# Retention then a bilinear FFN on one core: casts of two chunks moved ahead, four chunks of attention spread out, last rows stored in halves

## The chip, the core and the metric

One core of a Trainium2 chip runs the whole program. The metric is the device time of one execution in microseconds (us); the runs of the kernel before have a median of 350.2 us. A ratio below is the mean time of one kernel's fast runs over the mean of the other's fast runs of the same rounds, so it is not quite the ratio of the medians that are quoted. Spans in the profile (first to last instruction) are some 1.7 us shorter than the times.

Names used by the profile: PE is TensorE's matmuls, PEld its weight loads, DVE VectorE, ACT ScalarE, POOL GpSimd, SP SyncE, which issues most DMAs here. Tiles in its lines: qkb are q and k as bf16, tp and qkT their transposes, sc the scores, sT the masked scores, o the outputs of the attention, xT the FFN's input, pa and pb the FFN's first two products, po its last one, and osb the copy of po that is stored. A copy out of po is called an eviction.

## The reference

```python
def _attn_ref(q, k, v):                       # 8 batches, 8 heads, 576 positions, head size 64
    scores = np.matmul(q, k.transpose(0, 1, 3, 2)) / np.sqrt(64)
    rel = pos[:, None] - pos[None, :]
    Dmat = np.where(rel >= 0, gamma[:, None, None] ** rel[None], 0.0)   # decay, causal
    return np.matmul(scores * Dmat, v)

def _moe_ref(x, w_a, w_b, w_out):             # 4608 tokens, 512 -> 1536 -> 512
    return ((x @ w_a) * (x @ w_b)) @ w_out
```

The attention is linear (no softmax), so it can be done in chunks of 128 tokens with a running state: per chunk, `state` adds k'v to a matrix, `scores` makes q k' of the chunk itself, a mask job on DVE zeroes the non-causal half, `outputs` adds state and chunk, and an xT job on DVE scales the result into the FFN's input.

## The kernel before

The 36 chunks' attention is woven into the FFN's stream of matmuls. The FFN runs in blocks of tokens (512, 256, 384, 384, then 512 each); a generator yields after each matmul with its cost in units of a 512-column matmul, and the schedule runs its next entry when the running sum `at` has passed that entry's place and the stream is at an edge. Entries placed between edges slip to the next one: every 4 units in block 0's second half and in block 1's first, every 6 in the first half of the 384-token block.

```python
    def cast(i, on="pool"):              # q, k to bf16; v scaled to bf16
        ...
        if on == "pool": nc.gpsimd.tensor_copy(qb, qf)
        else:            nc.scalar.copy(qb, qf)
        if on == "dve":  nc.vector.tensor_copy(kb, kf)
        else:            nc.gpsimd.tensor_copy(kb, kf)
        ...
    def turn(i):                         # chunks 6 and up: q, k transposed by DMA, issued by SP
        ...
        nc.sync.dma_start_transpose(qkT..., natural[i][0]...)
    def transposes(i):                   # chunks 0 to 5: on TensorE, through PSUM
        ...
    def scores(i):
        ...
        later.append(lambda: masked(0))  # DVE jobs, run by pop() at places in the FFN's stream
        later.append(lambda: masked(1))
    ...
    def ahead(upto, on="pool"):
        while counts["cast"] <= min(upto, NCH - 1):
            i = counts["cast"]
            cast(i, on)
            counts["cast"] += 1
            if i >= FIRST_TURNED:                     # 6
                turn(i)
            if i >= FIRST_TURNED + 1 and counts["load"] < NCH:
                load(counts["load"])                  # q, k, v of a chunk 2 further on
                counts["load"] += 1

    def one_by_one(what, i):
        if what == "T":
            ahead(i, "dve")
            transposes(i)
        elif what == "S":
            scores(i)
            flush()
            state(i)
        else:
            flush()
            outputs(i)                                # leaves its xT job in `later`

    for i, first, second, third in ((4, 117, 122, 128), (5, 132, 135, 140)):
        todo += [(first, one_by_one, ("T", i)), (second, one_by_one, ("S", i)),
                 (third, one_by_one, ("A", i))]
    placed = [((6, 7), 145, 178, 194), ((8,), 166, 197, 207),
              ((9, 10), 186, 230, 250)]
    ...                                               # chunks 11 to 35: places worked back from
        placed.append((g, third - 104, third - 36, third))    # where their block starts
```

`later` is a list of DVE jobs; `pop()` starts one at the end of each pb group and twice per row block of po, `flush()` starts all. Each engine's queue is worked through in order: in the trace of before, the k cast of chunk 4 (48.37 us, its data there since 45.12) follows the eviction in front of it (47.76).

Of the kernel before, what the change touches and what calls it, by code (L numbers as in the profile page):

```python
# [10 lines left out]
FP32 = mybir.dt.float32  # L11
# [7 lines left out]
def kernel(  # L19
# [19 lines left out]
    nc = tc.nc  # L39

    B, H, S, D = q.shape
    DM = H * D
    DFF = moe_w_a.shape[1]
    NTOK = B * S
    NC = DM // 128
    NF = DFF // 128
# [10 lines left out]
    def rows_of(i):  # L57

        b, m = 2 * (i // PER), i % PER
        if m < MID:  # L60
            return [(0, 128, b, 128 * m)]
        if m == MID:
            return [(0, 64, b, 128 * m), (64, 64, b + 1, 0)]
        return [(0, 128, b + 1, 64 + 128 * (m - MID - 1))]

    def pool(name, bufs, space=None):
        kw = {} if space is None else {"space": space}
        return ctx.enter_context(tc.tile_pool(name=name, bufs=bufs, **kw))
# [11 lines left out]
    ps_ffn = pool("ps_ffn", 3, PS)  # L80
# [10 lines left out]
    wo_sb = big.tile([128, NF, DM], BF16)  # L91
# [18 lines left out]
    for i in range(4):  # L110
# [18 lines left out]
        out=mask, in_=mask, compare_op=ALU.is_ge, fill=0.0,  # L129
# [44 lines left out]
    def pop():  # L174
        if later:
            later.pop(0)()

    def flush():
        while later:
            later.pop(0)()  # L180
# [22 lines left out]
    def turn(i):  # L203

        qkT = qkt_pool.tile([128, 2, HP, 128], BF16, tag="qkT", name="qkT")
        nc.sync.dma_start_transpose(
            qkT.rearrange("p w c s -> p (w c) s"),
            natural[i][0].rearrange("p w d -> p (w d)"))
        transposed[i] = qkT

    def transposes(i):

        natural_qk = natural[i][1:3]
        qkT = qkt_pool.tile([128, 2, HP, 128], BF16, tag="qkT", name="qkT")
        for w, copy in ((0, nc.scalar.copy), (1, nc.vector.tensor_copy)):
            tp = ps_att.tile([128, HP, 128], BF16, tag="att", name="tp")
            for p in range(HP):
                nc.tensor.transpose(tp[:, p, :],  # L218
                                    natural_qk[w][:, p * 128:(p + 1) * 128],
                                    identity)  # L220
            copy(qkT[:, w], tp)
        transposed[i] = qkT
# [43 lines left out]
    def outputs(i, halves=False):  # L266
        m = i % PER
        qkb, qb, kb, vb = natural.pop(i)
        qkT = transposed.pop(i)
        sT = scored.pop(i)  # L270
        o = ps_att.tile([128, HP, 128], FP32, tag="att", name="o")
        if m > 0:
            st = state_of.pop(i)
            n = 64 if m == MID else 128
            for p in range(HP):
                for hi in (0, 1):
                    nc.tensor.matmul(o[64 * hi:64 * hi + 64, p, 0:n],  # L277
                                     st[:, p, 64 * hi:64 * hi + 64],
                                     qkT[:, 0, p, 0:n],
                                     start=(p == 0), stop=True,  # L280
                                     skip_group_check=True)
        for p in range(HP):
            for hi in (0, 1):
                e0 = p * 128 + 64 * hi
                nc.tensor.matmul(o[64 * hi:64 * hi + 64, p, :],  # L285
                                 vb[:, e0:e0 + 64], sT[:, hi, p, :],
                                 start=(m == 0 and p == 0), stop=True,
                                 skip_group_check=True)
        s0 = rows_of(i)[0][3]

        def scaled(c0, c1):
            nc.vector.tensor_tensor(  # L292
                xT[:, c0:c1, i * 128:(i + 1) * 128], o[:, c0:c1],
                qs[:, c0:c1, s0:s0 + 128], op=ALU.mult)

        if halves:
            later.append(lambda: scaled(0, HP // 2))
            later.append(lambda: scaled(HP // 2, HP))
        else:
            later.append(lambda: scaled(0, HP))  # L300
# [5 lines left out]
    def ffn_block(tok0, n, runs):  # L306

        hT = h_pool.tile([128, NF, 512], BF16, tag="h", name="hT")
        f0 = 0
        for count in runs:  # L310
            has = {}
            for F in range(f0, f0 + count):
                fs = slice(F * 128, (F + 1) * 128)
                pa = ps_ffn.tile([128, 512], FP32, tag="ab", name="pa")
                for c in range(NC):
                    nc.tensor.matmul(pa[:, 0:n], wa_sb[:, c, fs],  # L316
                                     xT[:, c, tok0:tok0 + n],
                                     start=(c == 0), stop=(c == NC - 1))
                    if c < NC - 1:
                        yield n / 512, False  # L320
                ha = ha_pool.tile([128, 512], BF16, tag="ha", name="ha")
                nc.scalar.copy(ha[:, 0:n], pa[:, 0:n])  # L322
                has[F] = ha
                yield n / 512, False
            for F in range(f0, f0 + count):
                fs = slice(F * 128, (F + 1) * 128)
                pb = ps_ffn.tile([128, 512], FP32, tag="ab", name="pb")
                for c in range(NC):
                    nc.tensor.matmul(pb[:, 0:n], wb_sb[:, c, fs],  # L329
                                     xT[:, c, tok0:tok0 + n],  # L330
                                     start=(c == 0), stop=(c == NC - 1))
                    if c < NC - 1:
                        yield n / 512, False
                nc.vector.tensor_tensor(hT[:, F, 0:n], has[F][:, 0:n],  # L334
                                        pb[:, 0:n], op=ALU.mult)
                pop()
                yield n / 512, True
            f0 += count
        for u in range(n // 128):
            po = ps_ffn.tile([128, 512], FP32, tag="ab", name="po")  # L340
            for F in range(NF):
                nc.tensor.matmul(po, hT[:, F, u * 128:(u + 1) * 128],  # L342
                                 wo_sb[:, F, :],
                                 start=(F == 0), stop=(F == NF - 1))
                if F == 5:
                    pop()
                if F < NF - 1:
                    yield 1.0, F % 4 == 3
            osb = o_pool.tile([128, DM], FP32, tag="osb", name="osb")
            if u % 2 == 0:  # L350
                nc.scalar.copy(osb, po)  # L351
            else:
                nc.vector.tensor_copy(osb, po)  # L353
            nc.sync.dma_start(
                out[tok0 + u * 128:tok0 + (u + 1) * 128, :], osb)
            pop()
            yield 1.0, True


    gate = const.tile([1, 64], BF16)  # L360
# [48 lines left out]
    starts, at = {}, 0.0  # L409
# [10 lines left out]
# [5 lines that stand above are left out]
            if i >= FIRST_TURNED:  # L425
                turn(i)
            if i >= FIRST_TURNED + 1 and counts["load"] < NCH:
                load(counts["load"])
                counts["load"] += 1
# [13 lines left out]
            outputs(i)  # L443

    def one_by_one(what, i):
        if what == "T":
            ahead(i, "dve")
            transposes(i)
        elif what == "S":
            scores(i)  # L450
            flush()
            state(i)
        else:
            flush()
            outputs(i)

    todo = []
    for i, first, second, third in ((4, 117, 122, 128), (5, 132, 135, 140)):
        todo += [(first, one_by_one, ("T", i)), (second, one_by_one, ("S", i)),
                 (third, one_by_one, ("A", i))]  # L460
    placed = [((6, 7), 145, 178, 194), ((8,), 166, 197, 207),
              ((9, 10), 186, 230, 250)]
    limit = 1e9
    for i in range(NCH - 1, 10, -2):
        g = (i, i + 1) if i + 1 < NCH else (i,)
        third = min(starts[i] - 16, limit - 60)
        limit = third
        placed.append((g, third - 104, third - 36, third))
    for g, zeroth, second, third in placed:
        todo += [(zeroth, ahead, (g[-1],)), (second - 14, first_stage, (g,)),  # L470
                 (second, second_stage, (g,)), (third, third_stage, (g,))]
# [2 lines left out]
    at = 0.0  # L474
    tok = 0
    for tb, n in enumerate(blocks):
        runs = WCOLS if tb == 0 else [1] * NF
        for cost, edge in ffn_block(tok, n, runs):
            at += cost
            while todo and edge and at >= todo[0][0]:  # L480
                _, fn, args = todo.pop(0)
                fn(*args)
        flush()
        tok += n
# [30 lines left out]
```

## Time and profile before

| of the kernel before | |
|---|---|
| time, median (lowest to highest of 4) | 350.22 us (350.19 to 352.2) |
| PE busy | 331.2 us of a span of 348.7 |
| start-up until the first FFN matmul | 21.66 us |
| from the end of the last matmul to the end of the span | 3.98 us |

The view by stretches of time shows where PE was not full. The columns are the stretch, its length, then busy us of PE, PEld, DVE, ACT and POOL with their numbers of instructions, the granted TensorE clock, the mean share of DMA engines busy (over 1 where packets overlap) and GB/s.

```profile
43.00:62.00 19.00, 15.53 (x134) 8.21 (x133) 7.53 (x14) 5.37 (x12) 8.09 (x11) 1.00 1.18 234
62.00:96.00 34.00, 31.97 (x325) 21.59 (x323) 18.75 (x35) 12.74 (x32) 12.72 (x17) 1.00 1.27 192
96.00:320.00 224.00, 224.00 (x1599) 111.81 (x1598) 106.11 (x166) 67.62 (x134) 49.23 (x65) 1.00 0.68 135
```

In the first row 3.5 us of PE are idle, in the second 2.0, in the third nothing in 224 us. The DMA share is above 1 in the first two rows and 0.68 in the third: the stretch with the holes is also the one in which the DMA engines are busy throughout.

### The profile page before, as it was taken

What the parts mean: (1) busy time and instruction counts of PE and PEld (TensorE: products, weight loads), DVE (VectorE), ACT (ScalarE), POOL (GpSimd) and SP (SyncE); (2) the same over time, 40 slices, a digit from 0 to 9 for tenths busy, and PEclk for the clock granted to TensorE, in tenths of its full rate; (3) what the DMA queues carried; (4) which work ended last, traced back from release to release, by engine and by line L of the source; (5) the groups of instructions that cost most, each with busy time, mean ns of one, the idle gap of its engine ahead of it and who ended that gap; (6) DMA issues with size and microseconds to landing.
All of it is one profiled execution on the core that took longest, in us unless ns stands there. A gap on an engine that the chain in (4) does not pass through costs nothing.

```text
span 348.7 us, 6143 instructions
## 1 busy us (share of the span) xinstructions
PE 331.2 (95%) x2414; PEld 170.7 (49%) x2414; DVE 160.9 (46%) x272; ACT 111.8 (32%) x228; POOL 85.0 (24%) x121
## 2 busy tenths in 40 slices
PE   2989987999799999999999999999999999999995
PEld 1544443866455654444444444444544444444442
DVE  5644334474664363365336533653365236513421
ACT  8522322514323342333142404240423143213320
POOL 4660035235333441220233023401331110000000
PEclk9999999999999999999999999999999999999999
DMA  9999999999999991930995099708990950020002
GB/s 175 191 196 208 206 209 250 211 201 187 186 220 232 218 229 62 212 59 3 223 264 116 2 204 268 133 0 160 251 196 0 155 149 2 0 92 30 0 32 90
DMA packets 154189, 50.74 MB, mean 146 GB/s; under 512 B 144944, under 2 KB 149552, under 8 KB 154160
## 3 DMA queue, kind: packets, MB, share of 16 engines
q1 hardware_dynamic: 149408, 45.63, 69.3%
q0 software_dynamic: 4752, 4.72, 8.4%
q8 instruction: 19, 0.31, 0.4%
q14 instruction: 10, 0.08, 0.1%
HBM read 37.75 MB, written 9.44 MB: 135 GB/s over the span
## 4 chain that ended last, share of the span: by engine, by line
PE 90%; DVE 3%; SPq 2%; POOL 2%; DMA 1%; issue 1%; ACT 0%; DVEq 0%
PE pa L316 27%; PE po L342 27%; PE pb L329 27%; PE o L277 2%; PE o L285 2%; SPq L104 2%; PE kv L235 2%; DMA vf<-in_v_dram 1%; DVE sT L258 1%; DVE hT L334 1%; POOL vb L196 1%; POOL wa_sb L163 1%; DVE xT L292 0%; POOL wb_sb L164 0%; DVE osb L353 0%
## 5 line engine op out<-in xcount | busy, mean ns | idle before, releaser
L334 DVE TENSOR_TENSOR hT<-ha,pb 128x512 bf16<-128x512 bf16 (+2 forms) x120 | 76.1, 634 | 107.3 <-PE pb L329 105.3
L316 PE MATMUL pa<-xT,wa_sb 128*128 128x512 bf16 (+2 forms) x480 | 111.7, 358 | 1.9 <-DVE xT L292 1.9
L329 PE MATMUL pb<-xT,wb_sb 128*128 128x512 bf16 (+2 forms) x480 | 111.5, 358 | 0.0
L322 ACT CAST ha<-pa 128x512 bf16<-128x512 f32 (+2 forms) x120 | 65.1, 542 | 125.7 <-PE pa L316 114.0
L342 PE MATMUL po<-wo_sb,hT 128*128 128x512 bf16 x432 | 98.0, 379 | 0.0
L329 PEld LDWEIGHTS <-wb_sb 128*128 128x128 bf16 x480 | 47.0, 98 | 46.5
L316 PEld LDWEIGHTS <-wa_sb 128*128 128x128 bf16 x480 | 45.1, 98 | 45.0 <-issue 2.2
L342 PEld LDWEIGHTS <-hT 128*128 128x128 bf16 x432 | 40.5, 98 | 47.1
L196 POOL TENSOR_TENSOR vb<-vf,vs 128x512 bf16<-128x512 f32 x36 | 37.5, 1042 | 58.9 <-DMA vf<-in_v_dram 44.8
L189 POOL CAST qkb<-qf 128x512 bf16<-128x512 f32 x30 | 18.3, 610 | 114.0 <-DMA qf<-in_q_dram 94.7
L353 DVE COPY osb<-po 128x512 f32<-128x512 f32 x17 | 11.8, 692 | 54.3 <-PE po L342 54.3
L351 ACT COPY osb<-po 128x512 f32<-128x512 f32 x19 | 11.1, 585 | 74.5 <-PE po L342 74.5
L292 DVE TENSOR_TENSOR xT<-o,qs 128x512 bf16<-128x512 f32 (+1 forms) x37 | 24.2, 671 | 9.5 <-PE o L285 9.2
L195 POOL CAST qkb<-kf 128x512 bf16<-128x512 f32 x32 | 19.6, 613 | 22.0 <-DMA kf<-in_k_dram 21.9
L285 PE MATMUL o<-sT,vb 128*64 128x128 bf16 x288 | 14.7, 222 | 1.3 <-DVE sT L258 1.3
L218 PE MATMUL tp<-identity,qkb 128*128 128x128 bf16 x48 | 5.6, 263 | 8.4 <-ACT qkb L191 6.8
L235 PE MATMUL kv<-vb,qkb 128*128 128x128 bf16 (+1 forms) x128 | 12.8, 224 | 0.7 <-POOL vb L196 0.7
L235 PEld LDWEIGHTS <-qkb 128*128 128x128 bf16 (+1 forms) x128 | 9.5, 99 | 7.1 <-issue 1.9
L285 PEld LDWEIGHTS <-vb 128*64 128x64 bf16 x288 | 10.3, 111 | 2.7 <-issue 2.3
L252 PEld LDWEIGHTS <-qkT 64*128 64x128 bf16 x288 | 8.6, 96 | 5.9 <-issue 1.9
L218 PEld LDWEIGHTS <-qkb 128*128 128x128 bf16 x48 | 3.8, 116 | 11.0 <-ACT qkb L191 7.6
L240 ACT CAST state_165<-kv 64x256 bf16<-64x256 f32 x8 | 2.9, 365 | 7.5 <-PE kv L235 7.5
(195 smaller groups left out, 155.4 us busy)
## 6 DMA issues: line engine op xcount, KB each, us to landing
out_dram<-osb SPq DMA_DIRECT2D x36, 256.0 KB, 3.1
qf<-in_q_dram SPq DMA_DIRECT2D x32, 256.0 KB, 4.0
kf<-in_k_dram SPq DMA_DIRECT2D x32, 256.0 KB, 4.6
vf<-in_v_dram SPq DMA_DIRECT2D x32, 256.0 KB, 4.9
wo_sb<-in_moe_w_out_dram POOLq DMA_DIRECT2D x3, 512.0 KB, 17.2
qf<-in_q_dram SPq DMA_DIRECT2D x8, 128.0 KB, 4.5
kf<-in_k_dram SPq DMA_DIRECT2D x8, 128.0 KB, 5.0
vf<-in_v_dram SPq DMA_DIRECT2D x8, 128.0 KB, 4.5
```

Of the source, the lines that this page charges most:

```text
L189: nc.gpsimd.tensor_copy(qb, qf)
L195: nc.gpsimd.tensor_copy(kb, kf)
L196: nc.gpsimd.tensor_tensor(vb.rearrange("p (h d) -> p h d", h=H), vf.rearrange("p (h d) -> p h d", h=H), vs[:, i % PER, :].unsqueeze(2).to_ ...
L235: nc.tensor.matmul(kv[:, p, :], kb[r, sl], vb[r, sl], start=(m in (0, MID) and p == 0), stop=True, skip_group_check=True)
L285: nc.tensor.matmul(o[64 * hi:64 * hi + 64, p, :], vb[:, e0:e0 + 64], sT[:, hi, p, :], start=(m == 0 and p == 0), stop=True, skip_group_che ...
L292: nc.vector.tensor_tensor(xT[:, c0:c1, i * 128:(i + 1) * 128], o[:, c0:c1], qs[:, c0:c1, s0:s0 + 128], op=ALU.mult)
L316: nc.tensor.matmul(pa[:, 0:n], wa_sb[:, c, fs], xT[:, c, tok0:tok0 + n], start=(c == 0), stop=(c == NC - 1))
L322: nc.scalar.copy(ha[:, 0:n], pa[:, 0:n])
L329: nc.tensor.matmul(pb[:, 0:n], wb_sb[:, c, fs], xT[:, c, tok0:tok0 + n], start=(c == 0), stop=(c == NC - 1))
L334: nc.vector.tensor_tensor(hT[:, F, 0:n], has[F][:, 0:n], pb[:, 0:n], op=ALU.mult)
L342: nc.tensor.matmul(po, hT[:, F, u * 128:(u + 1) * 128], wo_sb[:, F, :], start=(F == 0), stop=(F == NF - 1))
L353: nc.vector.tensor_copy(osb, po)
```

## The change

Its intent is to remove the known waits: casts ahead of the evictions that delayed them, the result of a single chunk evacuated at once, one more step of the FFN between scores and outputs of chunks 9 and 10 (so that the masks are ready), and a shorter tail. The core of the diff:

```diff
-            po = ps_ffn.tile([128, 512], FP32, tag="ab", name="po")
...
+            final = rows.stop == NTOK
+            for part in range(2 if final else 1):
+                cols = (slice(part * DM // 2, (part + 1) * DM // 2) if final
+                        else slice(0, DM))
...          # matmuls, eviction and store of `cols` alone; the last half is evicted by ScalarE
     def one_by_one(what, i):
-        if what == "T":
+        if what == "C":
             ahead(i, "dve")
+        elif what == "T":
             transposes(i)
...
             flush()
             outputs(i)
+            flush()
-    for i, first, second, third in ((4, 117, 122, 128), (5, 132, 135, 140)):
...
+    for i, places in ((4, (110, 117, 121, 127)), (5, (127, 132, 136, 139))):
+        todo += [(at, one_by_one, (what, i))
+                 for at, what in zip(places, "CTSA")]
...
-              ((9, 10), 186, 230, 250)]
+              ((9, 10), 186, 224, 254)]
...
-        placed.append((g, third - 104, third - 36, third))
+        placed.append((g, third - 104, third - (30 if i == 11 else 36), third))
```

More of the change, by code (lines that the diff above doesn't have):

```diff
@@ L339, in ffn_block @@
         for u in range(n // 128):
-            po = ps_ffn.tile([128, 512], FP32, tag="ab", name="po")
-            for F in range(NF):
-                nc.tensor.matmul(po, hT[:, F, u * 128:(u + 1) * 128],
-                                 wo_sb[:, F, :],
-                                 start=(F == 0), stop=(F == NF - 1))
-                if F == 5:
-                    pop()
-                if F < NF - 1:
-                    yield 1.0, F % 4 == 3
-            osb = o_pool.tile([128, DM], FP32, tag="osb", name="osb")
-            if u % 2 == 0:
-                nc.scalar.copy(osb, po)
-            else:
-                nc.vector.tensor_copy(osb, po)
-            nc.sync.dma_start(
-                out[tok0 + u * 128:tok0 + (u + 1) * 128, :], osb)
-            pop()
-            yield 1.0, True
+            rows = slice(tok0 + u * 128, tok0 + (u + 1) * 128)
+            final = rows.stop == NTOK
+            osb = o_pool.tile([128, DM], FP32, tag="osb", name="osb")
+            for part in range(2 if final else 1):
+                cols = (slice(part * DM // 2, (part + 1) * DM // 2) if final
+                        else slice(0, DM))
+                po = ps_ffn.tile([128, 512], FP32, tag="ab", name="po")
+                width = cols.stop - cols.start
+                for F in range(NF):
+                    nc.tensor.matmul(po[:, 0:width],
+                                     hT[:, F, u * 128:(u + 1) * 128],
+                                     wo_sb[:, F, cols],
+                                     start=(F == 0), stop=(F == NF - 1))
+                    if F == 5:
+                        pop()
+                    if F < NF - 1:
+                        yield width / 512, F % 4 == 3
+                if (u + part) % 2 == 0:
+                    nc.scalar.copy(osb[:, cols], po[:, 0:width])
+                else:
+                    nc.vector.tensor_copy(osb[:, cols], po[:, 0:width])
+                nc.sync.dma_start(out[rows, cols], osb[:, cols])
+                pop()
+                yield width / 512, True
     gate = const.tile([1, 64], BF16)
@@ L455, in one_by_one @@
             outputs(i)
+            flush()
     todo = []
-    for i, first, second, third in ((4, 117, 122, 128), (5, 132, 135, 140)):
-        todo += [(first, one_by_one, ("T", i)), (second, one_by_one, ("S", i)),
-                 (third, one_by_one, ("A", i))]
+    for i, places in ((4, (110, 117, 121, 127)), (5, (127, 132, 136, 139))):
+        todo += [(at, one_by_one, (what, i))
+                 for at, what in zip(places, "CTSA")]
     placed = [((6, 7), 145, 178, 194), ((8,), 166, 197, 207),
-              ((9, 10), 186, 230, 250)]
+              ((9, 10), 186, 224, 254)]
     limit = 1e9
```

## The prediction

> **What bounds the kernel now.** I read the page's busy shares and slices first, then the table of waits of TensorE (PE), then the order of time around each wait, then the DMA rows. The page:
>
> ```profile
> PE 331.2 (95%) x2414; PEld 170.7 (49%) x2414; DVE 160.9 (46%) x272; ACT 111.8 (32%) x228; POOL 85.0 (24%) x121
> ...
> PE   2989987999799999999999999999999999999995
> ...
> DMA  9999999999999991930995099708990950020002
> ```
>
> PE is the engine that bounds the kernel: full from about 96 us to the last slice, at the full granted clock. Its holes lie in the start-up, in slices 5 to 10 (44 to 96 us), and in the last slice. The DMA row is full until about 130 us, and that will matter. The waits of PE between 20 and 120 us:
>
> ```profile
> PE pa L316 <- DVE xT L292: 1.9, 2, 1.4
> PE o L285 <- DVE sT L258: 1.3, 3, 0.7
> PE tp L218 <- ACT qkb L191: 1.2, 1, 1.2
> PE tp L218 <- DVE qkb L193: 0.9, 1, 0.9
> PE sc_1389 L252 <- DVE xT L292: 0.7, 1, 0.7
> ```
>
> That is 6.0 us of idle PE, the whole reservoir of the scheduling part. Idle is measured from the modelled end of a matmul; from start to start, less the normal interval (0.216 us for 512 columns), the same holes lose more: 1.06 us (second transposes of chunk 4), 1.36 (transposes of chunk 5), 1.54 (first pa of block 1), 0.91+0.54 (outputs of chunk 10), 0.88 (scores of chunk 12), 0.68 (first pa of all), and 0.35 and 0.11; together 7.4 us after 20 us. I use these losses. Why the first three exist, in order of time:
>
> ```profile
> 47.76 0.69 DVE L353 COPY osb<-po 128x512 f32<-128x512 f32 x1 [4.42 <-PE po L342]
> 48.37 0.42 DVE L193 CAST qkb<-kf 128x512 bf16<-128x512 f32 x1
> 48.84 0.40 PE L218 MATMUL tp<-identity,qkb 128*128 128x128 bf16 x4 [0.90 <-DVE qkb L193]
> ...
> 53.26 0.58 ACT L351 COPY osb<-po 128x512 f32<-128x512 f32 x1 [1.82 <-PE po L342]
> 53.74 0.62 ACT L191 CAST qkb<-qf 128x512 bf16<-128x512 f32 x1
> 54.41 0.62 PE L218 MATMUL tp<-identity,qkb 128*128 128x128 bf16 x8 [1.20 <-ACT qkb L191]
> ...
> 59.00 0.69 DVE L353 COPY osb<-po 128x512 f32<-128x512 f32 x1 [1.45 <-PE po L342]
> 59.60 0.68 DVE L292 TENSOR_TENSOR xT<-o,qs 128x512 bf16<-128x512 f32 x1
> 60.34 0.60 PE L316 MATMUL pa<-xT,wa_sb 128*128 128x256 bf16 x4 [1.38 <-DVE xT L292]
> ```
>
> Each time a short job that PE needs at once (a cast, the last xT) sits in an in-order queue behind an eviction that itself waits for PE to finish a row of po. The cast's data was there long before: the records of landings have kf of chunk 4 at 45.12 us and of chunk 5 at 48.79.
>
> **What the Trainium skill says.** "Perfetto Trace Analysis", Identifying the Most-Contended Engine, warns that matmul busy share is no good measure of distance from roofline; so here, 95% busy hides losses larger than the idle time shown. Its section What "DMA-bound" means names, as one case, the issuing sequencer's track being solid DMA slices: the trace agrees, SyncE's issues follow each other from 36.8 to 95 us with gaps up to 0.6 us, and 144944 of 154189 packets are under 512 B. "TensorE: Matmul & The Clock Gate", Back-to-back issue gap, gives N/2.4+2.5 ns, so two 256-column matmuls (109 ns each) cost what one of 512 does (216); the trace agrees: four 256-column pa start every 0.43 us, weight loads included. "VectorE: DVE Perf Modes", The TRN2 errata, gives (172+N)/1.2 ns for ScalarE out of PSUM, 357 ns at 256 columns; the trace has 372 for the 256-column cast.
>
> **The change part by part.**
>
> *Casts ahead (chunks 4, 5).* The schedule acts only at multiples of 4 matmuls in this phase, so casts move from 120 to 112 and from 132 to 128; T, S and A stay at 120, 124, 128 and 132, 136, 140. Chunk 4: the k cast now precedes the eviction, runs near 45.3, and the 1.06 us goes. The next risk is the k copy of the transposes, behind the eviction: 48.45+0.42 = 48.85, when PE reaches the scores at 48.95. Chunk 5: ScalarE is free after the state copies (51.44, now 1.06 earlier), so q is cast by 51.0; DVE does xT of chunk 4 first (51.23 to 51.92), then the k cast to 52.25, needed at 52.20. So 1.36 shrinks to about 0.1.
>
> *Evacuated at once.* xT of chunk 5 no longer waits for the eviction of row block 3: outputs end about 55.64, xT at 56.35, PE needs it at 56.43. The 1.54 goes. Sum at the start of block 1: 1.06+1.26+1.54 = 3.9 us early (56.4 for 60.34).
>
> *Chunks 9 to 12.* Scores of 9 and 10 move from matmul 234 to 228, outputs from 252 to 258; both places fall on multiples of 6. Four mask jobs are popped one per step. Before, the fourth came only with the flush:
>
> ```profile
> 90.30 0.68 DVE L258 TENSOR_TENSOR sT<-sc_1232,mask 128x512 bf16<-128x512 f32 x1
> 90.44 0.22 PE L285 MATMUL o<-sT,vb 128*64 128x128 bf16 x1 [0.75 <-DVE sT L258]
> ```
>
> Now five steps (234 to 258) take four masks, each 0.56+0.68 us of DVE in a step of 1.30: 0.91+0.54 = 1.45 us goes. Scores of 11 and 12 move from 264 to 270, as far behind the outputs of 9 and 10 as before, so the 0.88 wait for xT stays by itself.
>
> *Last rows in halves.* PE time is the same (24 x 0.108 for 12 x 0.216). The tail is now eviction 0.69, issue and landing 2.00 (345.48 to 347.48, records of landings), end 1.2. The last eviction becomes ScalarE on 256 columns, about 0.37: -0.32. Half the bytes: the four stores of 56.8 us land 0.62 apart, so half a store is about 0.3 less at best; I take -0.25. Sum -0.57.
>
> Without anything else: 3.9+1.45+0.57 = 5.9 us.
>
> **What takes part of it back.** From chunk 6 on, qkT comes by DMA transposes, and that stream never waits for PE in this stretch: it runs solid from 36 us, so its landings stay where they are while PE comes earlier. Landings of qkT against the first scores before: chunk 6 65.17 against 68.83, 7 66.03 against 69.07, 10 81.71 against 84.50, and 12:
>
> ```profile
> 88.98 2.12 SPq L206 DMA_TRANSPOSE qkT<-qkb  x1
> 94.51 0.22 PE L252 MATMUL sc_1388<-qkT 64*128 64x128 bf16 x1
> ```
>
> It lands at 94.02, only 0.5 us ahead. In steps, with 0.1 us from landing to PE: (1) 3.9 early, chunk 7 would be wanted at 65.2 and comes at 66.13: 0.97 back, 2.94 left. (2) Chunk 10 is wanted at 80.26 (2.94 plus 1.30 for the earlier place) and comes at 81.81: 1.55 back, 1.4 left; then the 1.45 is won, 2.85. (3) Scores of chunk 12 are reached at about 92.9, come at 94.1, and pa goes on at 94.4. Before, pa went on at 95.77 with 6 matmul units fewer done, that is 97.07 for the same work: 2.65 us are left. The 0.88 wait for xT vanishes inside this one. After that qkT is 4.35 us ahead (chunk 14) or more, and PE is full, so 2.65 stays to the end. So DMA, not PE, decides there.
>
> Span 348.7 (the page's)-2.65-0.57 = 345.5; in time, 350.2-3.2 = 347.0 us (0.9% less).
>
> **The rivals.** *No cap:* were the transposes to come earlier along with PE (an engine's instruction fetches and the evictions' stores share the rings, and move), all 5.9 us would be won: 344.3. For it: stores precede the transposes on the queue. Against: the store of row block 3 was issued at 59.92, right behind its predecessor (59.83), its eviction done at 59.69, so that nothing waited for PE. *Cap bites harder:* if an instruction fetch falls before a needed transpose and delays it by 1 to 1.5 us (the DMA packets of the instruction queue show fetches at 70.6 and 85.9 us, and beside each two successive landings stand 2.5 apart instead of some 1.2), or casts disturb the block, some 1.2 us are left: 348.5. *DVE as the new bound in block 1:* hT plus mask is 0.42+0.69 in a step of 0.86, so earlier work piles up there; but nothing is added to it, only 0.35 us of loss stays. *The tail gives nothing*, if the landing is fixed latency: 347.3.
>
> **Range and chances.** The middle is set by one landing (94.02) and a tail term; run-to-run moves of landings of about 1 us and the rivals give 345.3 to 348.6. Faster by over 2% needs 7.0 us, more than all I count: 2%. Slower by 2%: 1%. Within: 97%.
>
> **What would show it.** In the new profile: tp without waits over 0.2 us; pa of block 1 starting near 56.4; no wait of o for sT at chunk 10; new waits of scores for the transposes (chunks 7, 10, 12), chunk 12 starting near 94.1; a last eviction of 0.37 us by ACT. Wrong it would be if scores of chunk 12 start well before 93 (more gain) or transposes land later than 94.5 (less).

## The result

The changed kernel took 346.42 us in the median of its first four runs, against 350.22: a ratio of 0.9874 (95% interval 0.983 to 0.992). Beside the last experiments it was measured again at 346.46 against 350.40 (0.9863). So it gained 3.8 to 3.9 us where 3.2 were predicted; it is faster, by less than 2%.

One of the first four runs took 879.55 us, and it was the profiled one. In it a 512-column matmul started mostly every 0.62 us, not every 0.216, with a granted clock of 1.0 on record. It was the only such run, nothing below uses it but a point of the last list, and its cause stays open. The profile after is that of a later fast run of the same kernel (span 344.9 us), here by the same stretches:

```profile
43.00:62.00 19.00, 18.49 (x166) 11.48 (x167) 9.46 (x18) 7.23 (x17) 8.33 (x11) 1.00 1.23 232
62.00:96.00 34.00, 31.38 (x306) 20.04 (x307) 18.10 (x34) 11.87 (x29) 12.58 (x18) 1.00 1.29 198
96.00:320.00 224.00, 221.85 (x1567) 111.32 (x1592) 106.40 (x167) 67.71 (x133) 49.23 (x65) 1.00 0.68 135
```

The first stretch won 3.0 us of PE; the second has more idle time than before, 2.6 us, although the mask waits in it were removed. (The third row's missing 2 us are matmul records lost from this trace, seen as single gaps of one matmul's length; its weight loads, 111.3 us, are as before.) The waits of PE between 20 and 120 us say what took their place (in total, times, longest):

```profile
PE sc L252 <- DMA qkT<-qkb: 2.3, 3, 1.3
PE pa L316 <- DVE xT L292: 0.5, 1, 0.5
PE tp L218 <- DVE qkb L193: 0.2, 1, 0.2
PE o L285 <- DVE sT L258: 0.2, 1, 0.2
PE po L349 <- issue: 0.2, 1, 0.2
```

All waits of the list before are gone or small (the 0.5 before pa lies in the start-up, as before), and one is new: scores wait for the DMA transposes. First, the removed ones in order of time, DVE's queue and then PE's first matmul of block 1:

```profile
51.06 0.69 DVE L292 TENSOR_TENSOR xT<-o,qs 128x512 bf16<-128x512 f32 x1 [0.47 <-PE o L285]
51.67 0.73 DVE L193 CAST qkb<-kf 128x512 bf16<-128x512 f32 x1
...
55.85 0.69 DVE L292 TENSOR_TENSOR xT<-o,qs 128x512 bf16<-128x512 f32 x1 [0.48 <-PE o L285]
56.82 0.69 DVE L360 COPY osb<-po 128x512 f32<-128x512 f32 x1 [0.27 <-PE po L349]
...
56.62 0.60 PE L316 MATMUL pa<-xT,wa_sb 128*128 128x256 bf16 x4
```

The last xT now comes before the eviction (osb), and block 1 starts at 56.62 us, 3.7 us earlier than the 60.34 of before, without a bracket behind its line, that is without a wait. Next, in the same view of all engines in order of time (SPq is SyncE's sequencer), the new wait at chunk 10 and at chunk 12, with the issue of chunk 12's transpose:

```profile
81.57 0.40 PE L252 MATMUL sc<-qkT 64*128 64x128 bf16 x8 [1.33 <-DMA qkT<-qkb]
...
88.68 2.06 SPq L206 DMA_TRANSPOSE qkT<-qkb  x1
...
92.45 0.40 PE L252 MATMUL sc<-qkT 64*128 64x128 bf16 x8
92.87 0.68 DVE L292 TENSOR_TENSOR xT<-o,qs 128x512 bf16<-128x512 f32 x1
93.56 0.45 PE L252 MATMUL sc<-qkT 64*128 64x128 bf16 x8 [0.71 <-DMA qkT<-qkb]
```

Chunk 11 is scored at 92.45, chunk 12 follows only at 93.56, 0.05 us behind the landing of its transpose (93.51 by the records of landings). The xT of chunk 10 ends at 93.55, at the same moment; two experiments below take these two apart. From there PE runs full to the end, and its last matmul ends at 341.62 us against 344.72.

### The profile page after: what moved, and what is told of

It reads as the page before. It is cut to its first block, busy times and chain, and to the rows that moved or that the text cites. A ratio compares the mean times of both kernels' runs of the same rounds, so it can differ in the third digit from the quotient of the medians.

```text
span 877.8 us, 6134 instructions
## 1 busy us (share of the span) xinstructions
PE 854.0 (97%) x2390; PEld 309.4 (35%) x2426; DVE 162.0 (18%) x272; ACT 112.6 (13%) x229; POOL 84.3 (10%) x121
## 4 chain that ended last, share of the span: by engine, by line
PE 97%; issue 2%; DMA 1%; SPq 0%; POOL 0%; DVE 0%; ACT 0%
PE pb L329 29%; PE pa L316 29%; PE po L349 28%; PE o L285 2%; PE kv L235 2%; PE o L277 2%; PE w L372 1%; PE tp L218 1%; DMA kf<-in_k_dram 1%; SPq L104 0%; POOL qkb L195 0%; PE sc_2460 L252 0%; PE sc_2449 L252 0%; PE sc_1402 L252 0%; PE sc_3677 L252 0%
## 5 line engine op out<-in xcount | busy, mean ns | idle before, releaser
L329 PE MATMUL pb<-xT,wb_sb 128*128 128x512 bf16 (+2 forms) x471 | 279.9, 775 | 2.7 <-issue 2.7
L316 PE MATMUL pa<-xT,wa_sb 128*128 128x512 bf16 (+2 forms) x472 | 277.3, 769 | 3.6 <-issue 3.1
L349 PE MATMUL po<-wo_sb,hT 128*128 128x512 bf16 (+1 forms) x425 | 253.2, 810 | 6.2 <-issue 6.2
L329 PEld LDWEIGHTS <-wb_sb 128*128 128x128 bf16 x480 | 82.8, 172 | 173.7 <-issue 168.0
L316 PEld LDWEIGHTS <-wa_sb 128*128 128x128 bf16 x480 | 80.7, 172 | 157.2 <-issue 151.4
L349 PEld LDWEIGHTS <-hT 128*128 128x128 bf16 x444 | 73.1, 169 | 162.1 <-issue 159.0
L360 DVE COPY osb<-po 128x512 f32<-128x512 f32 (+1 forms) x17 | 11.5, 676 | 175.5 <-PE po L349 175.5
L285 PE MATMUL o<-sT,vb 128*64 128x128 bf16 x288 | 30.4, 379 | 0.0
L235 PE MATMUL kv<-vb,qkb 128*128 128x128 bf16 (+1 forms) x128 | 25.4, 373 | 1.4 <-issue 0.9
L285 PEld LDWEIGHTS <-vb 128*64 128x64 bf16 x288 | 22.3, 181 | 2.5 <-issue 2.5
```

The lines of the kernel that those rows point to most:

```text
L235: nc.tensor.matmul(kv[:, p, :], kb[r, sl], vb[r, sl], start=(m in (0, MID) and p == 0), stop=True, skip_group_check=True)
L285: nc.tensor.matmul(o[64 * hi:64 * hi + 64, p, :], vb[:, e0:e0 + 64], sT[:, hi, p, :], start=(m == 0 and p == 0), stop=True, skip_group_che ...
L316: nc.tensor.matmul(pa[:, 0:n], wa_sb[:, c, fs], xT[:, c, tok0:tok0 + n], start=(c == 0), stop=(c == NC - 1))
L329: nc.tensor.matmul(pb[:, 0:n], wb_sb[:, c, fs], xT[:, c, tok0:tok0 + n], start=(c == 0), stop=(c == NC - 1))
L349: nc.tensor.matmul(po[:, 0:width], hT[:, F, u * 128:(u + 1) * 128], wo_sb[:, F, cols], start=(F == 0), stop=(F == NF - 1))
```

## The experiments

Landings are read from the DMA semaphores' records of each trace. Losses are from start to start, as in the prediction. All runs named here gave correct results, all profiles are of fast runs.

**The changed kernel again** (no edit).

> The changed kernel, unaltered, because the first profile of it fell in a very slow run. Theory (the DMA transposes cap the gain): span about 345 us, block 1 starting near 56.4 us, scores of chunks 7, 10 and 12 waiting for the landing of their transposed q and k, chunk 12 at about 94.1 us. Rival (no cap): those three waits are absent or under 0.2 us together. The three fast runs so far (346.0 to 346.5 us) are 0.6 us better than the theory's 347.0, so one of its terms must be off by that much; the trace should name it.

346.55 us (before: 350.26; ratio 0.9884). This trace happened to have a late start-up: its first FFN matmul came at 23.30 us, 1.8 later than in the trace shown above (21.51), and block 1 started at 58.10:

```profile
58.10 0.60 PE L316 MATMUL pa<-xT,wa_sb 128*128 128x256 bf16 x4
...
81.57 0.40 PE L252 MATMUL sc<-qkT 64*128 64x128 bf16 x8 [0.37 <-DMA qkT<-qkb]
```

At the scores of chunk 10 both traces are at 81.57, because both stood waiting for the same landing (81.52 in both), one for 1.49 us and one for 0.53, and both spans are 344.9. A whole 1.8 us of late start were absorbed in the waits. That is what a cap, a limit set by another stream of work, looks like. The kernel before seems to absorb none of it: 8 of its 42 runs here took 352.0 to 352.3 us, while the 13 fast runs of the changed kernel lie between 345.64 and 346.92. That those 8 had a late start is likely, but no trace of one is kept. The clause on chunk 7's wait failed in this trace: with the late start chunk 7 was not waited for.

**Each part alone.** Casts and evacuation alone (the kernel before with the `one_by_one` part of the diff and the new places of chunks 4 and 5):

> The kernel before with the casts ahead and the evacuation at once for chunks 4 and 5, nothing else. Both theories: block 1 starts 3.9 us earlier. Theory of the cap: chunk 12 (still at matmul 264) can't be scored before 94.1 us, pa goes on at 94.4 for 95.8 before, so only about 1.4 us of the 3.9 reach the end: some 348.8 us. Rival (no cap): 3.9 us reach the end, 346.3 us.

348.71 us, ratio 0.9965: 1.5 us of 3.9 by the median. Seven of its 22 runs took 350.05 to 351.47 us with a mean granted clock of 0.993 to 0.995; the other 15 took 347.85 to 349.31 at 0.998 to 1.0, the clock of every run of the kernel before. The median of these 15 is 348.43, 1.8 us of 3.9, and in the trace below, one of them, PE's last matmul ends 1.74 us earlier than before (342.98 for 344.72). Chunk 12, still at its old place, is reached 2.3 us before its data:

```profile
91.02 0.40 PE L252 MATMUL sc<-qkT 64*128 64x128 bf16 x8
93.70 0.40 PE L252 MATMUL sc<-qkT 64*128 64x128 bf16 x8 [2.28 <-DMA qkT<-qkb]
```

Places alone (the kernel before with the last two pairs of lines of the diff):

> The kernel before with the new places of chunks 9 to 12 alone. Both theories: the waits of the outputs of chunk 10 for its masks go (1.45 us), chunk 12 is reached at about 94.4 us, just behind its landing, and its own wait for xT of about 0.9 us stays: about 1.4 us gained, 348.8 us. A third idea, that the places are of no use by themselves: 350.2 us.

348.75 us, ratio 0.9958: 1.5 us, as expected, with the wait of 0.87 us for xT at chunk 12 still there.

Halves alone (the kernel before with the `part` loop of the diff):

> The kernel before with the last row block in two halves alone. Theory: a last eviction of 0.37 instead of 0.69 us and a landing 0.25 us sooner, 0.57 us in all: 349.65 us. Rival (the landing is a fixed latency): 0.3 us, 349.9 us. If the 0.6 us by which the whole change beat my middle lies here, it would be 1.2 us, 349.0 us.

349.59 us, ratio 0.9975. Its last eviction, which answers to the 0.69 us eviction by DVE that ends the trace of before:

```profile
344.56 0.37 ACT L358 COPY osb<-po 128x256 f32<-128x256 f32 x1 [2.03 <-DMA out_dram<-osb]
```

The eviction is 0.32 us shorter and the landing comes 1.73 us after the issue in place of 2.00, so both the theory's terms are there. From the last matmul's end to the span's end it is 3.32 us against 3.98: 0.66 us. The three parts add to 1.55 + 1.51 + 0.67 = 3.7 us by the medians, what the whole change gave, and to 4.0 with the 15 undisturbed runs of the first. That sum is no sign of independence: the first part alone would give 3.9 if it reached the end.

**Without the evacuation at once** (the changed kernel less the second `flush()`).

```diff
             outputs(i)
-            flush()
```

> The changed kernel without the evacuation at once. In the traces so far that part alone is worth about 1.5 us at the start of block 1. Theory of the cap: the scores of chunks 10 and 12 wait for their transposes anyway (0.53 and 0.90 us in the changed kernel's trace, which had a start-up 1.6 us late, so some 3 us in an ordinary run), the lost 1.5 us is hidden in these waits: 346.5 us, not more than 0.4 from the changed kernel. Rival (the gain of the early part reaches the end): 348.0 us.

346.30 us, ratio 0.988: no loss at all. In its trace block 1 waits 1.38 us for xT again, starting at 57.61, and chunk 10 and chunk 12 then wait 0.51 and 0.92 us for their landings (80.94 and 92.98):

```profile
57.61 0.60 PE L316 MATMUL pa<-xT,wa_sb 128*128 128x256 bf16 x4 [1.38 <-DVE xT L292]
...
93.03 0.41 PE L252 MATMUL sc<-qkT 64*128 64x128 bf16 x8 [0.76 <-DMA qkT<-qkb]
```

A part that removes 1.5 us of visible PE idleness is worth nothing at the end here. What sets the end is seen when three traces are put side by side: under the result, again, and here the first FFN matmul starts at 21.51, 23.30 and 21.37 us, block 1 at 56.62, 58.10 and 57.61, but chunk 12 lands at 93.51, 93.54 and 92.98, and the span ends 251.43, 251.38 and 251.38 us after that.

**The transpose of chunk 12 earlier, and later.** The first in `ahead`: the loads that follow chunk 11's cast are held until chunk 12's transpose is issued.

```diff
-            if i >= FIRST_TURNED + 1 and counts["load"] < NCH:
-                load(counts["load"])
-                counts["load"] += 1
+            if i >= FIRST_TURNED + 1 and i != 11:
+                for _ in range(2 if i == 12 else 1):
+                    if counts["load"] < NCH:
+                        load(counts["load"])
+                        counts["load"] += 1
```

> The changed kernel with the transpose of chunk 12 issued ahead of the loads of chunk 13. Both theories: its landing moves from 93.5 to some 90 us. Simple theory (the landing alone holds chunk 12): 0.9 us or more faster, 345.6 us. Finer theory: the second half of chunk 12's scores needs the bank that xT of chunk 10 frees, and that wait (0.88 us in the kernel before) ends at the same time as the landing, so the wait only changes its releaser from the DMA to VectorE: 346.3 us, within 0.3 of the changed kernel.

346.37 us, ratio 0.9879: nothing gained, with the landing at 89.57, 3.7 us before chunk 12 is wanted. The finer theory holds: PE goes into chunk 12 (9 matmuls in a row) and stops where the bank is not free.

```profile
93.01 0.45 PE L252 MATMUL sc<-qkT 64*128 64x128 bf16 x9
93.44 0.68 DVE L292 TENSOR_TENSOR xT<-o,qs 128x512 bf16<-128x512 f32 x1
...
94.18 0.39 PE L252 MATMUL sc<-qkT 64*128 64x128 bf16 x7 [0.72 <-DVE xT L292]
```

So at chunk 12 two waits ended together, and to take away one alone does nothing. This run cannot show what the landing costs by itself, also because chunk 10 waited 1.62 us in it. The other direction can: the transpose of chunk 12 behind the loads of chunk 14.

```diff
-            if i >= FIRST_TURNED:
+            if i >= FIRST_TURNED and i != 12:
                 turn(i)
             ...
+            if i == 12:
+                turn(i)
```

> The changed kernel with the transpose of chunk 12 issued behind the loads of chunk 14. Landing some 3.4 us later, at about 97 us. Theory of the cap: PE waits one for one, 3.4 us slower: 350.0 us, as slow as the kernel before. Rival (the landing of chunk 12 does not set the end): within 0.5 us of 346.5.

351.63 us, ratio 1.0035: slower than the kernel before, and by 1.6 us more than expected. The landing was at 96.62 and PE waited 4.28 us for it, so the one-for-one part is right. The rest is in the matmuls behind it: here the span ends 253.05 us after the landing, 1.7 more than in the three traces above. First two windows, the wait and the 4.4 us after it:

```profile
92.30:96.60 4.30, 0.09 (x4) 0.00 (x0) 0.79 (x2) 0.52 (x2) 2.85 (x4) 1.00 1.34 226
96.60:101.00 4.40, 4.33 (x23) 2.20 (x24) 1.16 (x2) 0.65 (x2) 0.42 (x1) 0.61 1.24 218
```

Then PE's matmuls in order of time:

```profile
97.00 1.46 PE L316 MATMUL pa<-xT,wa_sb 128*128 128x384 bf16 x4
...
101.28 0.81 PE L316 MATMUL pa<-xT,wa_sb 128*128 128x384 bf16 x4
```

The granted clock fell to 0.61 in the mean of the second window (0.5 for 3.4 us in the record of the clock), and a 384-column matmul started every 0.32 us at the worst, not 0.162: eleven steps took 3.47 us in place of 1.79, which is the 1.7 us. The Trainium skill has this: "TensorE: Matmul & The Clock Gate", Why this matters for your kernels, warns of idle gaps over about 3 us, after which the array runs at half its clock. This trace agrees, with 0.5 on record after a wait of 4.28 us. The wait of 2.28 us in the trace of the casts alone left the clock at 1.0; that seven other runs of that kernel show a lower mean clock fits a longer wait at the same place, but no trace of one is kept.

**Later places for chunks 9 to 14.** If PE stands where it need not, let it do FFN work first.

```diff
-              ((9, 10), 186, 224, 254)]
+              ((9, 10), 186, 230, 262)]
...
-        placed.append((g, third - 104, third - (30 if i == 11 else 36), third))
+        placed.append((g, third - 104, third - (30 if i == 13 else 36), third))
+    placed[-1] = ((11, 12), 192, 282, 302)
```

> The changed kernel with the attention of chunks 9 to 14 placed later still: outputs of 9 and 10 at matmul 264, scores at 234; scores of 11 and 12 at 282, outputs at 304; scores of 13 and 14 at 330. Theory of the cap: nothing is computed less, but PE works ahead where it waited; what stays is the first part (3.3 us up to chunk 10 in the trace with the casts alone), 1.45 (masks), 0.88 (xT before the scores of chunk 12) and 0.66 (tail): 6.0 to 6.3 us, about 344.3 us, faster than the changed kernel by 2 us. If the start-up is 1.6 us late as in its trace, up to 345.5. Rival: the waits are not what sets the end; 346.5 us, or slower, as the later outputs wait for masks.

344.92 us, ratio 0.9838, with 4 runs from 344.28 to 345.14: the mechanism is right and the gain some 0.6 us smaller than expected. Its trace has waits of 0.49, 0.21 and 0.20 us at chunks 7, 8 and 10; at chunk 12 none. Its first FFN matmul starts at 21.44 us, no later than elsewhere, so that the start-up does not explain the 0.6. So three more were run side by side with more rounds: the changed kernel, the later places (both without an edit), and the later places with the casts and evacuation of the kernel before (the `one_by_one` part of the change undone):

> The changed kernel once more, to stand beside the next two on the same chip: 346.5 us, the first wait of over 0.2 us after block 0 at the scores of chunk 7, 8 or 10 if its start-up is not late this time, and 0.9 us at chunk 12.

> The later places of chunks 9 to 14 once more, beside the changed kernel: 344.9 us, 1.5 us faster than it.

> The later places of chunks 9 to 14 with the old casts and the old evacuation of chunks 4 and 5. Theory of the cap: with the cap lifted, the early part's 3.9 us count, less the 0.9 us that the later places still wait at chunks 7, 8 and 10: 3.0 us slower than with the new casts, 347.9 us. In the changed kernel itself the same part is worth only 1.5 us (places and halves alone add to 2.15 us of its 3.7). Rival (the early part is worth its 1.5 us wherever it stands): 346.4 us.

The changed kernel came to 346.46 us (0.9863; its trace is the one shown under the result), the later places to 344.11 (0.9802, interval 0.977 to 0.983), 2.35 us faster than the changed kernel in the same rounds, where 1.5 were expected. The waits of the kernel with later places:

```profile
PE pa L316 <- DVE xT L292: 0.5, 1, 0.5
PE sc L252 <- DMA qkT<-qkb: 0.2, 1, 0.2
```

The wait for the transposes is down from 2.3 us to 0.2, with the same DMA stream: its chunk 12 landed at 92.86 and was scored at 93.22. With the old casts under the later places the time was 347.36 us (0.9907): the same first part of the change that gave 1.5 to 1.8 us on the kernel before gives 3.25 us here, where the cap is lifted (3.0 were expected). The rival's 346.4 is refuted, as no run of this kernel was below 347.13. What the part is worth inside the changed kernel itself was not run; the 1.5 us of the expectation is a difference of sums.

## Why the prediction was right

The time (346.4 to 346.6 for 347.0), its range and the class all hold. Point by point, for the trace shown above:

| step | predicted | measured |
|---|---|---|
| second transposes of chunk 4 | loss goes | no wait |
| transposes of chunk 5 | 0.1 us left | 0.40 (the k cast took 0.73 us in this trace); at most 0.23 in the other traces with these casts |
| start of block 1 | 56.4 us | 56.62 |
| chunk 7 waits for its transpose | 0.97 us | 0.45, and 0.16 at chunk 8 |
| chunk 10 waits for its transpose | 1.55 us, at 81.81 | 1.49, at 81.57 |
| outputs of chunk 10 wait for masks | loss of 1.45 us goes | no wait |
| chunk 12 starts | 94.1 us | 93.56 |
| gain left on PE at the end | 2.65 us | 3.10 (344.72 to 341.62) |
| tail | 0.57 us | 0.66 (3.98 to 3.32) |

The statement that decided it, "DMA, not PE, decides there", is what the experiments show most plainly: 1.5 us removed from or added to the early part changes nothing (no evacuation at once, late start-up), a later landing adds its delay, and later places without any faster work gain 2.35 us. "The 0.88 wait for xT vanishes inside this one" is right as well, with a sharper meaning than I gave it: the two waits end within 0.1 us of each other, and xT would hold PE there if the landing did not.

The middle was 0.5 us too high. The mis-sized terms are the landing of chunk 12, taken as 94.02 from one trace, and the 0.1 us from landing to PE: the landing was 93.51 and the way to PE 0.05, together 0.56 us, of which 0.1 was lost again between these scores and the next pa (0.38 us, not 0.3); the tail term was short by 0.1. The size of the waits before chunk 12 played no part: those at chunks 7, 8 and 10 add to 2.1 us in the trace of the result and to 0.5 in the one with the late start, and both end alike. With the 251.4 us from landing to end found above, a landing at 94.02 would have given a span of 345.4, and the prediction had 345.5. The landing is not a fixed number. In traces with the same order of DMAs it was 92.40, 92.86, 92.98, 93.48, 93.51, 93.54, 93.58, 93.66, 94.02 and 94.81 us; the first was a kernel whose PE in this stretch was that of before. The prediction allowed about 1 us for this. Why it moves was not tested.

The rivals: "no cap" (344.3) is refuted for the changed kernel, but is nearly the time of the version with later places. Its premise failed too: the eviction of block 0's last rows was done at 57.51 in place of 59.69, but their store was still issued at 59.83 (59.92 before), and the transposes of chunks 6, 7, 10 and 12 behind it landed only 0.2 to 0.5 us earlier. What the prediction says of shared rings holds for the stores alone: the DMA records have the 19 fetches of 16 KB on queue 8 and SyncE's transfers on queue 1. "Cap bites harder" did not happen, though fetches of instructions do lie beside the gaps in landings; whether they cause them no run tested. "DVE as the new bound in block 1": the 0.35 us loss stayed as it was. "The tail gives nothing" beyond the eviction is refuted by the halves alone.

Not tested: the casts of chunks 4 and 5 without the evacuation at once, in the kernel before; places and halves together without the casts.

## What to carry to other kernels

When a wait of the bounding engine is removed, ask what it will run into when it comes earlier: list, for each later hand-over, how long the data had lain there, and cap the gain at the slack of a stream that does not come earlier with it, plus the waits behind that hand-over which vanish in the new one. Where that stream is the limit, moving its consumer later, behind work that is ready, gains more than making anything faster. Two waits that end at the same moment hide each other; test each by moving it in the direction that hurts.

## What the Trainium skill lacked or had wrong

- "DMA: Bandwidth & Descriptors", DMA Transpose (X-bar), lists constraints but no time of issue, and another section of that page has only sequencer cycles of earlier generations for other sizes and paths: a transpose of one chunk's q and k (128 rows of 1024 bf16, SBUF to SBUF) held SyncE's sequencer 1.28 to 2.38 us, median 1.98, in the trace of before, against some 0.57 for an undisturbed load, and landed 3.2 to 6.5 us after its issue.
- No page of those I read gives the sustained rate of loads in 256-byte pieces issued from SyncE: here successive 256 KB landings stand about 1.16 us apart between 44 and 58 us, some 226 GB/s as worked out from that.
- "Runtime: NRT & Kernel Launch", Instruction fetch mechanics, says that instructions are refilled in blocks of 16 KiB through a DMA queue and that the cost is mostly hidden, but not what a refill costs the data transfers beside it: 19 fetches of 16 KB appear in the DMA packets of before, and beside those at 70.6 and 85.9 us landings stand 2.5 us apart. That the fetches cause it is not shown.
- "TensorE: Matmul & The Clock Gate", Part 1, says that the records of the clock gate can be unreliable and that the gate has been seen stuck low for over 50 us. The 879.55 us run, with 0.62 us for most 512-column matmuls and 1.0 on record, may be such a case, but nothing shows that the gate was its cause. The page has no case that lasts a whole run.
- The same page's warning about idle gaps over some 3 us is right here: a wait of 4.28 us halved the clock for 3.4 us and cost about 1.7 us more.
